# First four chunks turned by float32 identity products on TensorE in place of DMA transposes, state sums in float32, re-timed order

## The chip, the cores and the metric

The kernel runs on one core of a Trainium2 chip. The metric is the device time of one execution in microseconds (us). Engine names are those of the profile: PE (TensorE, the matrix unit; PEld its weight loads), DVE (VectorE), ACT (ScalarE), POOL (GpSimd), SP (SyncE, which here issues all DMA transfers).

## The reference

A gated linear attention is followed by a gated expert layer.

```python
for t in range(S):                                    # 4 batches, 8 heads, S = 768, D = 48
    state = alpha[:, :, t, :, None] * state + einsum('bhd,bhde->...', k[t], v[t])
    y[:, :, t] = einsum('bhd,bhde->bhe', q[:, :, t], state)
x = y as [3072 tokens, 384]
xn = x / sqrt(mean(x * x) + 1e-6) * rms_g
out = (silu(xn @ w_gate) * (xn @ w_val)) @ w_out      # 384 -> 1536 -> 384
```

All inputs and outputs are float32. (The first einsum is shortened here: it is the outer product of k and v of one token.)

## The kernel before

**Tiling.** The 3072 tokens are 24 chunks of 128. Chunk `cc` is the `cc // 4`-th chunk in time of batch `cc % 4`, so chunks 0 to 3 are the first chunks of the four batches: they have no state before them (`first`), and their output needs no product with a state. Seven groups (`GROUPS`: 4, 2, 2, 4, 4, 4, 4 chunks) go through the expert layer together.

**Attention of one chunk** (`attention`). SP loads decays, q and k of the chunk (`att`, 112 rows: two heads of 48, at rows 0 and 64) and v. DVE runs two scans over the decays (`scan`), and multiplies k and q by the results (`kh`, `qp`). PE multiplies k and q into scores (`sc`), DVE masks them (`mask`), PE multiplies them with v (`y32` for the first four chunks, in float32; `yv` later). ACT sums the squares (`sq`), POOL takes the root (`pow`), DVE multiplies by the gain (`x`), ACT and DVE split the scaled x into a high and a low float16 part (`x16`, `xl`). A DMA transpose on SP (`x_turn`) turns both parts into `xT`, which the expert layer multiplies. For the state, k is split into float16 parts as well (`k16`, `kl`), turned by a DMA transpose (`k_turn`), and multiplied with the float16 parts of v (`v16`, `vl`) by 48 small products on PE (`sums`).

**Float32 by float16 pairs.** Nearly every product is made of three float16 products (high x high, high x low, low x high: `SPLIT`). The low part is a subtraction on DVE.

**Weights.** 12 tiles of w_gate and w_val (`i0` to `i11`) and 6 of w_out (`o0` to `o5`) are loaded, brought into form by ACT (`abs`) and DVE (`shift`, `rest`), and split: the high part on ACT (`wh`), the low part on DVE (`wl`). For the names in `LOW_W` the low part is made by PE instead: two float32 products with a scaled identity (`wid`), two with minus the identity (`wneg`), and a copy by ACT (`wl2`).

**Expert layer.** `expert_in` makes 18 products per tile and column block (9 for gate, 9 for value); `expert_out` makes 36 per chunk. In group 0 the first five tiles (`EARLY`) are first multiplied with chunks 0 and 1 alone (256 columns), then with chunks 2 and 3 (`CUTS`); the names in the order are `mm_<group>_<tile>_<first chunk>_<gate 0 or value 1>`.

**Order.** No loop sets the order. Each piece of work is an `op` with an engine, a planned cost (`COST`) and a due time; the class `Plan` lays them out by a list schedule, with buffer counts (`BUFS`: one `y` output bank, three `at` and three `mm` banks, three row buffers `att`, two raw weight buffers), and the code is then written in that order, engine by engine. Each engine executes its queue in order. The tables `DUE`, `GAP`, `LATE` and `W_LATE` shift due times and so set the order.

**Row loads.** `load_att` fills a row buffer with one transfer of 112 rows the first time, and later with two of 48 rows, leaving the padding rows as they are.

## Time and profile before

| | us |
|---|---|
| device time, three runs | 532.52, 533.43, 533.54 (median 533.43) |
| device time of the profiled execution | 532.83 |
| span of the profiled execution | 531.0 |
| PE busy in the span | 505.1 (95%) |
| DVE busy | 395.1 (74%) |
| ACT busy | 259.3 (49%) |
| POOL busy | 34.7 (7%) |

The span is what lies between the first and the last instruction in the profile. A busy share is an average over stages: here the first 68 us, the stretch from there to 523 us, and the last 7.6 us differ, and the stages are shown with the prediction. A view of groups gives, for the instructions of one line and shape, the count, the busy time, the mean time of one in ns, and the idle time before them with what ended it; a timeline gives them in order of time; a table of waits gives for each engine whom it waited for, in total, how often and the longest. The granted clock is that of PE, 1.00 being full.

### The profile page before, as it was taken

The page shows a single profiled execution, that of the slowest core. Times are in us where ns is not written, and L with a number is a line of the kernel's source. Part 1 is how long each engine was busy: PE and PEld are TensorE (multiplying, and loading weights), DVE is VectorE, ACT ScalarE, POOL GpSimd, SP SyncE. Part 2 cuts the span into 40 slices and gives each one's busy share as a digit, 9 for nine tenths or more (in the row PEclk, how much of TensorE's full clock was granted, in tenths as well). Part 3 has the DMA queues.
Part 4 walks back from the last instruction along what each step waited for, and adds up shares of the span by engine and source line. Part 5 has one row for each costly group of instructions (what it writes and reads, how often), then busy time and mean ns, then how long its engine had stood idle before and what let it go on. Part 6 is the DMA issues. An engine that isn't in the chain of part 4 may idle for free.

```text
span 531.0 us, 11900 instructions
## 1 busy us (share of the span) xinstructions
PE 505.1 (95%) x4798; PEld 301.4 (57%) x4798; DVE 395.1 (74%) x745; ACT 259.3 (49%) x674; POOL 34.7 (7%) x79
## 2 busy tenths in 40 slices
PE   2888999999999999999999999999999999999994
PEld 1656774567886886545556545456544456444551
DVE  7997999999999999999997779898644320333212
ACT  3565888744663574446734557665544310232200
POOL 3002000001001010100210000021100000000000
PEclk9975999999999999999999999999999999999998
DMA  8999976748346539453379992516710000000001
GB/s 263 215 243 225 192 222 197 222 95 160 61 75 152 94 75 141 110 93 63 78 185 243 234 215 75 190 32 156 209 54 1 15 16 31 15 1 1 1 34 32
DMA packets 70673, 62.65 MB, mean 118 GB/s; under 512 B 40257, under 2 KB 64961, under 8 KB 70609
## 3 DMA queue, kind: packets, MB, share of 16 engines
q1 hardware_dynamic: 70608, 61.81, 50.8%
q8 instruction: 39, 0.64, 0.5%
q14 instruction: 26, 0.20, 0.1%
HBM read 47.77 MB, written 4.72 MB: 99 GB/s over the span
## 4 chain that ended last, share of the span: by engine, by line
PE 78%; DVE 11%; DMA 3%; ACT 1%; issue 1%; DVEq 0%
PE mm L1078 47%; PE mm_po L1148 22%; PE at L756 2%; DMA kT<-k 2%; PE y L841 2%; PE at L896 2%; DVE w L649 1%; PE y L820 1%; DVE wu_i L543 1%; DVE h L1108 1%; DVE h L1095 1%; DMA xT<-x 1%; DVE wu_o L543 1%; PE y_i L558 1%; DVE wg L551 1%
## 5 line engine op out<-in xcount | busy, mean ns | idle before, releaser
L1078 PE MATMUL mm<-xT,wg 128*128 128x512 f16 (+1 forms) x1602 | 291.6, 341 | 0.5 <-ACT sl L1089 0.2
L1078 PEld LDWEIGHTS <-wg 128*128 128x128 f16 x1602 | 155.3, 99 | 122.4 <-issue 0.5
L1148 PE MATMUL mm_po<-wo,h 128*128 128x384 f16 x864 | 144.9, 326 | 0.3 <-DVE ob L1159 0.3
L1148 PEld LDWEIGHTS <-h 128*128 128x128 f16 x864 | 83.0, 98 | 55.8 <-issue 1.3
L1095 DVE SCALAR_TENSOR_TENSOR h<-mm,sl 128x512 f32<-128x512 f32 (+1 forms) x89 | 52.1, 586 | 46.6 <-PE mm L1078 45.1
L503 ACT ACTIVATE h<-h 128x512 f16<-128x512 f32 (+1 forms) x89 | 48.6, 547 | 77.8 <-DVE h L1095 77.4
L1089 ACT ACTIVATE sl<-mm 128x512 f32<-128x512 f32 (+1 forms) x89 | 45.5, 512 | 45.9 <-PE mm L1078 45.3
L1108 DVE TENSOR_TENSOR h<-h,h 128x512 f16<-128x512 f32 (+1 forms) x89 | 51.7, 585 | 18.9 <-ACT h L503 18.7
L649 DVE TENSOR_TENSOR_SCAN w<-att,seed 112x520 f32<-112x520 f32 x48 | 59.4, 1238 | 2.7 <-DMA att<-att 2.3
L1159 DVE TENSOR_SCALAR ob<-mm_po 128x384 f32<-128x384 f32 x24 | 13.3, 554 | 34.9 <-PE mm_po L1148 34.9
L935 POOL TENSOR_TENSOR ss<-ssq,eps 128x1 f32<-128x1 f32 x24 | 12.0, 501 | 371.3 <-ACT junk L931 371.3
L769 DVE TENSOR_TENSOR at<-at,mask 128x512 f32<-128x512 f32 x40 | 25.9, 692 | 4.4 <-PE at L756 4.0
L880 ACT CAST a<-at 128x512 f16<-128x512 f32 x40 | 22.9, 584 | 10.1 <-DVE at L769 9.9
L883 DVE TENSOR_TENSOR a<-at,a 128x512 f16<-128x512 f32 x40 | 25.8, 684 | 0.1
L503 ACT ACTIVATE k<-kh 112x512 f16<-112x512 f32 x24 | 15.1, 627 | 9.7 <-DVE kh L679 7.3
L503 ACT ACTIVATE q<-qp 112x512 f16<-112x512 f32 x20 | 12.6, 628 | 13.5 <-DVE qp L686 9.9
L686 DVE TENSOR_TENSOR qp<-att,w 112x256 f32<-112x256 f32 x48 | 18.8, 420 | 0.1
L945 ACT ACTIVATE x<-x,ss 128x384 f16<-128x384 f32 x24 | 14.7, 611 | 5.0 <-POOL ss L936 3.5
L936 POOL TENSOR_TENSOR ss<-ss,mhalf 128x1 f32<-128x1 f32 x24 | 16.9, 706 | 1.9
L756 PE MATMUL at<-q,k 48*128 48x128 f16 x480 | 16.9, 217 | 0.0
L693 DVE TENSOR_TENSOR k<-kh,k 112x512 f16<-112x512 f32 x24 | 16.4, 682 | 0.7 <-ACT k L503 0.7
L503 ACT ACTIVATION_READ_ACCUMULATOR h<-h 128x1 f32 x89 | 16.8, 188 | 0.0
(107 smaller groups left out, 433.4 us busy)
## 6 DMA issues: line engine op xcount, KB each, us to landing
att<-att SPq DMA_DIRECT2D x42, 289.9 KB, 5.1
v<-vtok SPq DMA_DIRECT2D x24, 192.0 KB, 3.4
out_dram<-ob SPq DMA_DIRECT2D x24, 192.0 KB, 2.2
raw_c<-w_gate SPq DMA_DIRECT2D x12, 384.0 KB, 4.7
raw_c<-w_val SPq DMA_DIRECT2D x12, 384.0 KB, 5.6
raw_d<-w_out SPq DMA_DIRECT2D x6, 768.0 KB, 5.6
raw_i<-w_gate SPq DMA_DIRECT2D x11, 384.0 KB, 7.0
raw_i<-w_val SPq DMA_DIRECT2D x11, 384.0 KB, 8.4
```

The lines of the kernel that those rows point to most:

```text
L503: nc.scalar.activation(dst, src, AF.Copy, scale=scale, accum_out=stat[:rows, col : col + 1])
L649: nc.vector.tensor_tensor_scan(w, x, start.rearrange("r g p c -> r (g p c)"), 0.0, op0=ALU.mult, op1=ALU.add)
L686: nc.vector.tensor_tensor(by_half(t["qp"])[:, g], q, w, op=ALU.mult)
L756: nc.tensor.matmul(o, t["k16"][r, x, p, :], t["q16"][r, y, p, :], start=m == 0, stop=m == 2,)
L769: nc.vector.tensor_tensor(t["sc"][j], t["sc"][j], mask[:, int(first)].to_broadcast([P, NP, C]), op=ALU.mult,)
L880: nc.scalar.copy(a_tile()[:, j, 0], t["sc"][j])
L883: nc.vector.tensor_tensor(a_tile()[:, j, 1], t["sc"][j], a_tile()[:, j, 0], op=ALU.subtract)
L1078: nc.tensor.matmul(ps[:, :n], wg[:, f, x, j, kk, :], xT[:, y, kk, cs], start=i == 0, stop=i == 3 * NK - 1,)
L1089: nc.scalar.activation(t["sl"][:, :n], t[0][:, :n], AF.Silu, scale=1.0 / (S_X * S_W))
L1095: nc.vector.scalar_tensor_tensor(t["h"][:, :n], t[1][:, :n], S_H / (S_X * S_W), t["sl"][:, :n], op0=ALU.mult, op1=ALU.mult,)
L1108: nc.vector.tensor_tensor(h16_of(g, f)[:, 1, cs], t["h"][:, :n], h16_of(g, f)[:, 0, cs], op=ALU.subtract)
L1148: nc.tensor.matmul(t[i][:, :DM], h16_of(g, f)[:, x, ts], wo[:, f // 2, y, f % 2, :], start=f == 0 and m == 0, stop=f == NF - 1 and m == 2,)
```

## The change

For chunks 0 to 3 (`first`):

- k is no longer split. PE multiplies each of the four pairs of heads of `kh` with a float32 identity (`kp`: four products, 112 rows to 128 x 112), ACT copies the result (`k16`, now a float32 copy into the `kT` buffer), and the state sums are 16 float32 products with v itself (`u32`) in place of 48 float16 ones. The splits of v fall away too.
- x is scaled by root and gain in one DVE operation (`scaled`, which now waits for POOL's root), turned by three float32 products with the identity (`xp`, into an `mm` bank), and split on the way out: ACT copies the high part into `xT` (`x16`), DVE subtracts it for the low part (`xt`).
- So eight DMA transposes go, four of k and four of x.

For all chunks, the rows are loaded in one transfer of 112 rows. `LOW_W` keeps `i0` and `i1`; the low parts of `i2` and `i3` return to DVE. The tables of due times have new numbers. A new constant `one` (identity) is made on POOL, and start values of the check statistics change.

```diff
-LOW_W = ("i0", "i1", "i2", "i3")
+LOW_W = ("i0", "i1")
@@
-GAP = [-27.4, 83.2, 75.1, 36.9, -13.6, -70.1, 64.4]
+GAP = [-30.6, 131.5, 92.4, 44.6, -25.7, -125.5, 179.1]
...
     def load_att(cc, lo, hi):
-        new = (plan.slot["att", cc], lo) not in held
-        held.add((plan.slot["att", cc], lo))
-        for r in (slice(0, R),) if new or hi - lo < AW else (slice(0, D), slice(64, R)):
-            nc.sync.dma_start(att_tile(cc)[r, lo:hi], att[src(cc), r, lo:hi])
+        nc.sync.dma_start(att_tile(cc)[:, lo:hi], att[src(cc), :, lo:hi])
@@
+        def k_across():
+            t["kp"] = buf(ps_at, [P, NP, R], F32, "at", (cc, 4))
+            for p in range(NP):
+                nc.tensor.matmul(t["kp"][:, p, :], t["kh"][:, p, :], one[:R, :R], start=True, stop=True)
+
+        def k_back():
+            k = tl(ap, [P, 2, NP, R], F16, "kT").rearrange("s x p r -> s (x p r)").bitcast(F32)
+            t["k32"] = k.rearrange("s (p r) -> s p r", p=NP)
+            nc.scalar.copy(t["k32"], t["kp"])
+
+        def sums32():
+            t["u"] = [buf(ps_at, [R, NP, D], F32, "at", (cc, 2 + h)) for h in range(2)]
+            v = tiles["v", cc].rearrange("s (j p e) -> s j p e", j=2, p=NP)
+            for p in range(NP):
+                for j in range(2):
+                    r = slice(64 * j, 64 if j == 0 else R)
+                    for h in range(2):
+                        rows = slice(h * HC, (h + 1) * HC)
+                        nc.tensor.matmul(
+                            t["u"][h][r, p, :], t["k32"][rows, p, r], v[rows, j, p, :],
+                            start=True, stop=True,
+                        )
@@
+        def scaled():
+            t["x32"] = tl(ap, [P, DM], F32, "x32")
+            nc.vector.scalar_tensor_tensor(
+                like(t["x32"]), y_sum(), t["ss"], like(rg), op0=ALU.mult, op1=ALU.mult
+            )
+
+        def x_across():
+            t["xp"] = buf(ps_mm, [P, NK, C], F32, "mm", key("x"))
+            for kk in range(NK):
+                nc.tensor.matmul(
+                    t["xp"][:, kk, :], t["x32"][:, kk * P : (kk + 1) * P], one, start=True, stop=True
+                )
+
+        def x_half(x):
+            o = xT_of(g)[:, :, :, i * C : (i + 1) * C]
+            if x == 0:
+                nc.scalar.copy(o[:, 0], t["xp"])
+            else:
+                nc.vector.tensor_tensor(o[:, 1], t["xp"], o[:, 0], op=ALU.subtract)
@@
+        if first:
+            xp = ("mm", key("x"))
+            x = add("DVE", "x", scaled, [rt, tiles["rg"]], [y_k, key("x32"), key("ss")])
+            x = add("PE", "xp", x_across, [x], [key("x32"), xp])
+            x = add("ACT", "x16", lambda: x_half(0), [x], [xp, ("xT", g)])
+            xt = op("DVE", COST["xl"], lambda: x_half(1), [x], [xp, ("xT", g)], due=due, kind="xt")
@@
             if first:
+                kt = add("PE", "kp", k_across, [kh], [key("kh"), u2])
+                kt = add("ACT", "k16", k_back, [kt], [key("kT"), u2])
+                u = add("PE", "u32", sums32, [kt, lv], [key("kT"), key("v"), u0, u1])
                 st = add("ACT", "st0", s_back, [u], [u0])
```

Where the instructions stand now. In the rows, the number behind a name is the chunk (or the weight tile), the last one only counts the tiles.

**DVE, up to the operation that the first expert product waits for.** Before, the rows end with the multiply of chunk 2 (`x32_2`), which frees the one `y` bank for chunk 3's output on PE:

```order
L693 TENSOR_TENSOR k16_3_397<-kh_3_393,k16_3_397 112x512
L543 SCALAR_TENSOR_TENSOR wu_i8_414<-raw_i8_256,wu_i8_414 128x768
L649 SCALAR_TENSOR_TENSOR w_4_422<-att1_142,seed_91 112x520
L551 SCALAR_TENSOR_TENSOR wg_133<-wu_i8_414,wg_133 128x768
L783 TENSOR_TENSOR a16_3_440<-at_3_0_404,mask_97 128x512
L783 TENSOR_TENSOR a16_3_440<-at_3_1_405,mask_97 128x512
L727 SCALAR_TENSOR_TENSOR gd_4_443<-dec_132 112x4
L669 RECIPROCAL seed2_95<-w_4_422 112x8
L738 TENSOR_TENSOR sd0_349<-st0_348,gd_4_443 112x192
L711 SCALAR_TENSOR_TENSOR v16_3_434<-v_3_342,v16_3_434 128x384
L941 TENSOR_TENSOR x32_2_500<-y_2_425,rg_90 128x384
```

After the change, they end with the subtract that completes the turned x of chunk 1 (`xT_0` is the turned x of group 0; `mm_x_1` the bank into which PE turned chunk 1):

```order
L663 RECIPROCAL seed2_95<-w_4_345 112x8
L721 SCALAR_TENSOR_TENSOR gd_4_364<-dec_139 112x4
L732 TENSOR_TENSOR sd0_286<-st0_285,gd_4_364 112x192
L962 SCALAR_TENSOR_TENSOR x32_1_376<-y_1_325,ss_1_361,rg_90 128x384
L777 TENSOR_TENSOR a16_3_379<-at_3_0_347,mask_97 128x512
L777 TENSOR_TENSOR a16_3_379<-at_3_1_348,mask_97 128x512
L545 SCALAR_TENSOR_TENSOR wg_140<-wu_i2_341,wg_140 128x768
L643 SCALAR_TENSOR_TENSOR w_4_345<-att_4_216,seed2_95 112x520
L534 TENSOR_SCALAR wu_i5_415<-raw_i5_292 128x768
L537 SCALAR_TENSOR_TENSOR wu_i5_415<-raw_i5_292,wu_i5_415 128x768
L978 TENSOR_TENSOR xT_0_318<-mm_x_1_392,xT_0_318 128x3x128
```

The low parts of k (`k16`) and v (`v16`) are gone, chunk 3 has overtaken chunk 2, and both scans of chunk 4 (`w_4`) stand ahead of the gate, where it was one.

**PE, among the first expert products.** Before, the state sums of chunk 3 from the DMA-turned k (`kT_3`) stand between the first and the second product group:

```order
L1078 LDWEIGHTS wg_133
L1078 MATMUL mm_0_0_0_0_532<-xT_0_266,wg_133 128x256
L896 LDWEIGHTS kT_3_420
L896 MATMUL at_3_2_549<-v16_3_434,kT_3_420 64x48
L896 LDWEIGHTS kT_3_420
L896 MATMUL at_3_3_550<-v16_3_434,kT_3_420 64x48
```

After the change, behind the fifth product group, the turning of chunk 3's x and the output of chunk 2:

```order
L1126 MATMUL mm_0_2_0_0_515<-xT_0_318,wg_140 128x256
L969 MATMUL mm_x_3_535<-one_111,x32_3_526 128x128 x3
L790 MATMUL y_2_543<-v_2_457,a16_2_331 128x48 x8
L1126 LDWEIGHTS wg_140
L1126 MATMUL mm_0_2_0_1_565<-xT_0_318,wg_140 128x256
```

and behind three more groups the state sums of chunk 1, the turning of chunk 2's k and x:

```order
L899 MATMUL at_1_2_609<-v_1_157,kT_1_277 48x48
L899 MATMUL at_1_3_610<-v_1_157,kT_1_277 48x48
L884 MATMUL at_2_4_633<-one_111,kh_2_289 128x112 x4
L969 MATMUL mm_x_2_645<-one_111,x32_2_627 128x128 x3
L1126 LDWEIGHTS wg_140
L1126 MATMUL mm_0_4_0_0_656<-xT_0_318,wg_140 128x256
```

The state sums of chunk 2 follow two product groups later. Chunk 3's output, which stood right ahead of the first product, still does.

**SP, the queue of transfers.** Before, from the loads of chunk 2's rows on:

```order
L432 DMA att2_159<-att 112x1546
L432 DMA att0_137<-att 48x1546 x2
L697 DMA_TRANSPOSE kT_0_189<-k16_0_179 128x8x112
L432 DMA att1_142<-att 48x1546 x2
L529 DMA raw_i2_220<-w_gate 128x3x1024
L529 DMA raw_i2_220<-w_val 128x3x1024
L697 DMA_TRANSPOSE kT_1_234<-k16_1_214 128x8x112
L437 DMA v_2_245<-vtok 128x384
L529 DMA raw_i8_256<-w_gate 128x3x1024
L529 DMA raw_i8_256<-w_val 128x3x1024
L959 DMA_TRANSPOSE xT_0_266<-x16_0_251 128x6x128
```

After the change:

```order
L423 DMA att_1_150<-att 112x522
L423 DMA att_2_152<-att 112x1546
L423 DMA att_1_150<-att 112x1024
L428 DMA v_1_157<-vtok 128x384
L523 DMA raw_i0_159<-w_gate 128x3x1024
L523 DMA raw_i0_159<-w_val 128x3x1024
L523 DMA raw_i1_165<-w_gate 128x3x1024
L523 DMA raw_i1_165<-w_val 128x3x1024
L423 DMA att_3_183<-att 112x1546
L423 DMA att_4_216<-att 112x1546
L523 DMA raw_i2_250<-w_gate 128x3x1024
L523 DMA raw_i2_250<-w_val 128x3x1024
```

Chunk 2's rows now stand ahead of the first two weight tiles, and no transpose stands between the loads.

More of the change, by code (lines that the diff above doesn't have):

```diff
@@ L92 @@
 W_LATE = [
[L93 to L94 removed]
+    -228.4, -155.3, -67.5, 59.0, 68.2, 5.4, 63.1, 136.0, 18.2, 137.7, 147.9, 35.5, 44.8, 167.4,
+    194.4, 105.4, 241.9, 186.0,
 ]
@@ L419, in att_tile @@
     def att_tile(cc):
-        n = plan.slot["att", cc]
-        return tile_of(
-            ("att", n),
-            lambda: ain.tile([R, AW], F32, tag=f"att{n}", name=f"att{n}", bufs=1),
-        )
-    held = set()
+        return tile_of(("att", cc), lambda: buf(ain, [R, AW], F32, "att", cc))
     def load_att(cc, lo, hi):
-        new = (plan.slot["att", cc], lo) not in held
-        held.add((plan.slot["att", cc], lo))
-        for r in (slice(0, R),) if new or hi - lo < AW else (slice(0, D), slice(64, R)):
-            nc.sync.dma_start(att_tile(cc)[r, lo:hi], att[src(cc), r, lo:hi])
+        nc.sync.dma_start(att_tile(cc)[:, lo:hi], att[src(cc), :, lo:hi])
     def load_v(cc):
@@ L471, in tile_attn_moe @@
     same = const.tile([P, P], F32, name="same")
+    one = const.tile([P, P], F32, name="one")
     nc.gpsimd.memset(same, 0.0)
-    for x, value in ((minus, -1.0), (same, S_W)):
+    nc.gpsimd.memset(one, 0.0)
+    for x, value in ((minus, -1.0), (one, 1.0), (same, S_W)):
         nc.gpsimd.affine_select(
@@ L495, in tile_attn_moe @@
     nc.gpsimd.memset(stat, 0.0)
-    nc.gpsimd.memset(stat[:, o_qq : o_qq + NB], 2.0**10)
+    for o in (0, o_kk, o_qq):
+        nc.gpsimd.memset(stat[:, o : o + NB], 2.0**14)
     ssq = const.tile([P, NC], F32, name="ssq")
@@ L920, in s_front @@
             nc.vector.scalar_tensor_tensor(
-                st, t["u"][1], S_K[1] / S_K[0], st, op0=ALU.mult, op1=ALU.add
+                st, t["u"][1], S_K[1] / S_K[0] * (S_V if first else 1.0), st, op0=ALU.mult, op1=ALU.add
             )
@@ L982, in attention @@
         qp = add("DVE", "qh", lambda: mul_q(1), [qp], [att_k, w_k, key("qp")], lock=True)
-        kd = add("ACT", "k16", k_hi, [kh], [key("kh"), key("k16")])
-        kl = add("DVE", "kl", k_lo, [kd], [key("kh"), key("k16")], lock=True)
-        vd = add("ACT", "v16", v_hi, [lv], [key("v"), key("v16")])
-        vl = add("DVE", "vl", v_lo, [vd], [key("v"), key("v16")], lock=True)
+        if not first:
+            kd = add("ACT", "k16", k_hi, [kh], [key("kh"), key("k16")])
+            kl = add("DVE", "kl", k_lo, [kd], [key("kh"), key("k16")], lock=True)
+            vd = add("ACT", "v16", v_hi, [lv], [key("v"), key("v16")])
+            vl = add("DVE", "vl", v_lo, [vd], [key("v"), key("v16")], lock=True)
         if first:
```

39 lines of the change are left out of this document (19 added, 20 removed).

## The prediction

> **What bounds the kernel now.** I first cut the span into stages, at the places where TensorE (PE) changes its state. Each row gives the stretch, its length, then busy us and instruction count of PE, PE weight loads, DVE, ACT and POOL, the granted clock, the DMA share and the GB/s.
>
> ```profile
> 0.00:44.64 44.64, 28.22 (x243) 21.80 (x244) 38.59 (x66) 22.29 (x51) 7.35 (x32) 0.86 1.05 231
> 44.64:68.02 23.38, 21.91 (x253) 16.81 (x254) 19.34 (x38) 17.10 (x46) 2.17 (x2) 0.82 1.04 219
> 68.02:101.20 33.18, 33.18 (x187) 17.52 (x182) 32.41 (x55) 26.84 (x63) 0.74 (x2) 1.00 0.69 205
> 101.20:130.80 29.60, 29.22 (x409) 19.08 (x409) 29.21 (x55) 14.22 (x37) 1.22 (x3) 1.00 0.71 145
> 130.80:523.40 392.60, 392.59 (x3716) 226.22 (x3715) 274.97 (x534) 178.87 (x479) 23.26 (x41) 1.00 0.40 91
> 523.40:531.00 7.60, 0.00 (x0) 0.00 (x0) 0.56 (x1) 0.00 (x0) 0.00 (x0) 0.76 0.13 38
> ```
>
> From 68 to 523 us PE is never free: the idle time is 0.4 us in 455, at full clock. That stretch can only move as a block. What can change is when it starts, and how much PE work it holds. The 26 us in which PE does nothing lie in the first 68 us (17.9) and behind the last product (7.6). DVE is nearly as full from 68 to 131 us (61.6 of 62.8), so it stands right behind PE.
>
> Next come the waits of PE in the first stages, and PE's own timeline there (start, us, instruction, idle before).
>
> ```profile
> PE y L796 <- DVE x L941: 2.0, 1, 2.0
> PE at L896 <- DMA kT<-k: 1.1, 1, 1.1
> ...
> 35.59 1.99 PE L796 MATMUL y<-v,a 128*128 128x48 f32 x16
> 38.67 0.54 PE L896 MATMUL at<-v,kT 64*64 64x48 f16 x47 [0.96 <-DVE a L783]
> 41.19 3.65 PE L796 MATMUL y<-v,a 128*128 128x48 f32 x16 [1.98 <-DVE x L941]
> 44.64 2.12 PE L1078 MATMUL mm<-xT,wg 128*128 128x256 f16 x9
> 47.85 0.83 PE L896 MATMUL at<-v,kT 64*64 64x48 f16 x48 [1.09 <-DMA kT<-k]
> 48.61 5.21 PE L1078 MATMUL mm<-xT,wg 128*128 128x256 f16 x27
> 53.66 1.46 PE L558 MATMUL y_i<-wu_i,same 128*128 128x384 f32 x4
> 54.95 0.49 PE L565 MATMUL y_i<-wg,minus 128*128 128x384 f16 x2
> 68.02 33.25 PE L1078 MATMUL mm<-xT,wg 128*128 128x256 f16 x180
> ```
>
> The first expert product is at 44.64. It stands behind chunk 3's output (41.19), which waits for DVE's multiply of chunk 2 to free the one output bank. At 47.85 PE waits for the transposed k of chunk 3: the only place where a transpose holds PE.
>
> The clock (stretch, PE busy, granted clock, DMA share, GB/s):
>
> ```profile
> 44.00:46.00 2.00, 2.00 (x11) 0.50 1.98 191
> ...
> 52.00:54.00 2.00, 2.00 (x14) 0.77 1.13 205
> 54.00:56.00 2.00, 2.00 (x13) 1.00 1.18 142
> ```
>
> So the first products run at half clock until about 53 (0.77 in 52 to 54 is about 0.9 us at half; the 27 records from 48.61 take 0.193 each). From 44.64 that is some 8.4 us, of which half, 4.2 us, is lost.
>
> **The change, part by part.** The sum is made on the profiled run: span 531.0 us, 532.83 us with what lies around it. The median shown, 533.43, is 0.6 above that.
>
> *1. The first product comes earlier.* DVE fills the time ahead of it. Its two ends, and the mean times of what leaves or joins its queue (busy us, mean ns, idle):
>
> ```profile
> 3.96 1.31 DVE L649 TENSOR_TENSOR_SCAN w<-att,seed 112x520 f32<-112x520 f32 x1 [2.34 <-DMA att<-att]
> 40.58 0.56 DVE L941 TENSOR_TENSOR x<-y,rg 128x384 f32<-128x384 f32 x1 [0.43 <-ACT junk L931]
> ...
> L649 DVE TENSOR_TENSOR_SCAN w<-att,seed 112x520 f32<-112x520 f32 x48 | 59.4, 1238 | 2.7 <-DMA att<-att 2.3
> L693 DVE TENSOR_TENSOR k<-kh,k 112x512 f16<-112x512 f32 x24 | 16.4, 682 | 0.7 <-ACT k L503 0.7
> L948 DVE SCALAR_TENSOR_TENSOR x<-x,ss,x 128x384 f16<-128x384 f32 x24 | 14.7, 611 | 1.3 <-ACT x L945 1.2
> L711 DVE SCALAR_TENSOR_TENSOR v<-v,v 128x384 f16<-128x384 f32 x24 | 13.2, 551 | 0.0
> L941 DVE TENSOR_TENSOR x<-y,rg 128x384 f32<-128x384 f32 x10 | 5.5, 554 | 0.8 <-ACT junk L931 0.8
> ```
>
> Before, DVE gates the first product with the multiply that ends at 41.14 (57th operation in its queue). After, the gate is the subtract that completes the turned x of chunk 1 (51st). Counted in the two queues up to there, three low parts of k (0.68 each) and three of v (0.55) are gone, one multiply (0.55) falls behind the gate, one scan (1.24) comes ahead of it; two low parts of x become two subtracts, taken at the same 0.61. That is 2.0 + 1.7 + 0.55 - 1.24 = 3.0 us less, so the subtract ends at 38.1. Chunk 3's output now stands ahead of the gate in both queues (its masks are six operations earlier on DVE), so the product follows at once, where before it came 3.5 us behind the multiply.
>
> Against that stand new waits: the turned x goes DVE, PE, ACT, DVE, and while the subtract waits, chunk 4's scaled q and k and the next weight tiles stand behind it on DVE; on PE the scores of the next chunk stand behind a product that waits for DVE's x. Bounds: 0, and 3.65, what one cold output pass of PE takes (41.19). I take 1.2, nearer the low end, since other work stands between the steps in each queue. First product at 39.3: **5.3 us earlier**.
>
> *2. The wait for kT goes:* **1.1 us** (47.85). Late next on PE is the scaled x of chunk 3, which the order places behind five half-size expert products.
>
> *3. PE work behind the first product.* Before, three state sums (two here, one later) and a weight tile by PE: 0.5 + 0.5 and 1.46 + 0.49 less overlap (53.66 to 55.4), 2.8 us. After: two turned x, one turned k, two float32 state sums, and chunk 2's output. The trace has no such shapes; the nearest float32 rows are the output above (1.99 us for 16 records, 0.124 each, 48 columns) and the weight tile:
>
> ```profile
> 32.69 1.56 PE L558 MATMUL y_i<-wu_i,same 128*128 128x384 f32 x4
> 34.50 1.16 PE L764 MATMUL at<-qp,kh 48*128 48x128 f32 x16
> ```
>
> that is 0.39 per record at 384 columns, and 0.073 where two quarter-height tiles run side by side. A turned x is three products, six records of 128 columns: between 0.75 and 2.3 us; 1.0, since 128 lies nearer 48. A turned k, eight records of 112: between 1.0 and 3.1; 1.2. A state sum, 32 records on quarter tiles: between 0.36 (at the 0.011 of 38.67) and 2.3 (at 0.073); 1.0, between the f16 form of the same tiles and the next float32 one. Chunk 2's output is 2.0. Sum 2.0 + 1.2 + 2.0 + 2.0 = 7.2, less 2.8: **4.4 us more** (bounds 2.4 and, everything dear, 11.5).
>
> *4. Clock:* half clock for some 8.4 us around the first products, as before: **0**. The order puts a turned x and an output of 48 columns among them (the profile went to 0.50 right after such outputs, 35.59 and 38.67), so I don't count on less.
>
> *5. Hidden or small.* ACT trades the high parts of k and v of four chunks, and two residues, for copies of like size, and is half free (22.29 of 44.64). POOL makes one more constant before the first turned k, under the first scores; if late, only that product waits. The row loads grow from two of 48 rows to one of 112:
>
> ```profile
> att<-att SPq DMA_DIRECT2D x42, 289.9 KB, 5.1
> v<-vtok SPq DMA_DIRECT2D x24, 192.0 KB, 3.4
> att<-att SPq DMA_DIRECT2D x1, 676.4 KB, 10.7
> xT<-x SPq DMA_TRANSPOSE x24, 2.8
> kT<-k SPq DMA_TRANSPOSE x20, 4.7
> ```
>
> 676.4 - 2 x 289.9 = 97 KB more per chunk, five chunks of it in the first 60 us: 0.5 MB, 2 us at 231 GB/s. Seven transposes (by their shapes 229 KB for k, 197 for x) leave the same stretch, 1.5 MB. So the DMA engines, at a share over 1 until 68, get relief. On SP the chunk loads wait for one of three row buffers with weight loads behind them: before, it is the transposes that stand there. Weight loads can land late where the row load ahead of them is held; bounds 0 and 3 us, taken 0, since the bytes fall. After 131 us the share is 0.40 and all of this is covered.
>
> [...] The medians agree roughly (4.7 us against 3.4 for v); the chain's own piece does not:
>
> ```profile
> 35.76 12.04 DMA kT<-k
> ```
>
> [...]
>
> **Sum:** -5.3 - 1.1 + 4.4 + 0 = -2.0. 532.83 becomes 530.8; on the median, 531.4. I forecast 531.0, between the two.
>
> **Rivals.** *(a) DVE hands the gain back: no change.* Up to the gate of the last in-product of group 0, DVE's queue is only 0.9 us shorter (155 against 152 operations), because two weight tiles' low parts return to it. The order moves the low part of weight tile i10 from 122nd to 138th, 11.1 us of DVE work later. Before, it was ready long ahead:
>
> ```profile
> 80.50 0.93 DVE L551 SCALAR_TENSOR_TENSOR wg<-wu_i,wg 128x768 f16<-128x768 f32 x1
> 405.27 23.31 PE mm L1078 x108
> ```
>
> ready at 81.4, used 36 products of 0.216 before 101.2, at 93.4. After: 92.5, if DVE idles as much as before. Then PE can gain 0.9 at most, whatever its start: 532.2. For it speaks DVE's 61.6 of 62.8 us; against, that 4.0 us of DVE idle in 44.64 to 68.02 sit beside the waits that go.
>
> *(b) The clock stays half: slower.* If the turned x and the output among the first products keep the clock at 0.50 until 58, 9.4 us are lost in place of 4.2: -2.0 + 5.1 = +3.1, 536. It turns slower from 52 us on. For it: a pass of such outputs went before each drop to half. Against: at 49 to 53 us of before, dense products brought the clock back. Dear float32 records (term 3's upper ends) give the same size.
>
> *(c) The clock is full early: faster.* If PE, now denser ahead of 39 us, enters the products at full clock, the 4.2 us come back; DVE's queue allows 4.0 + 0.9 in all. 528.0. [...] The trace had 8.4 us from the first product to full clock, so I give it little.
>
> *(d) The change doesn't cut what PE waits for:* the turned k leaves only 1.1 us of PE waits, so if the earlier start fails, terms 2 and 3 give +3.3. It counts with (b).
>
> **How the numbers follow.** Forecast 0.46; (a) 0.21; (b) with (d) 0.20; (c) 0.13. A measurement of this kernel can tell about 0.2%, 1.1 us, from no change. Faster by more: forecast and (c), and a little of (a): 0.62. Within: the rest of (a): 0.18. Slower: 0.20. The range goes from 527.5 (just past (c)) to 535.5 (most of (b)); what lies outside is less than 2 in 10.
>
> **What would show it.** Right: a first expert product at 38 to 40.5, no wait of PE for a DMA of kT, a block without PE idle from about 60 on; a turned x near 1.0 and a turned k near 1.2 us at full clock; DVE idle between 40 and 65 under 3 us. Wrong: PE waiting for DVE's low part of a weight tile around 85 to 95 us (a); a granted clock of 0.50 past 52 us (b), or 1.00 at the first product (c); DVE waiting for raw weight loads (term 5); PE idle behind 130 us.

## The result and the profile after

The changed kernel took **527.13 us** (median of 5 runs, 526.57 to 528.63), against 532.52 us (531.49 to 533.54) for the kernel before on the same chip: a ratio of 0.9902, 95% interval 0.9879 to 0.9925. The profiled run took 526.98 us with a span of 525.3 us; before, 532.83 and 531.0. So the change brought about 5.4 us where 2.0 were forecast.

The stages after, cut where TensorE (PE) changes its state as in the prediction's first view (stretch, length, busy us of PE, weight loads, DVE, ACT and POOL, granted clock, DMA share, GB/s):

```profile
0.00:38.93 38.93, 27.44 (x225) 22.99 (x226) 32.62 (x54) 14.79 (x32) 10.00 (x34) 1.00 0.98 246
38.93:57.51 18.58, 16.48 (x192) 13.60 (x192) 18.37 (x35) 14.57 (x39) 2.56 (x4) 1.00 0.80 230
57.51:86.87 29.36, 29.36 (x185) 17.53 (x182) 28.80 (x51) 24.40 (x64) 0.00 (x0) 1.00 0.76 214
86.87:124.64 37.77, 36.95 (x448) 22.11 (x448) 37.04 (x67) 19.44 (x47) 1.48 (x4) 1.00 0.59 146
124.64:518.00 393.36, 393.36 (x3738) 227.78 (x3739) 275.25 (x535) 178.82 (x480) 18.85 (x41) 1.00 0.36 94
```

PE's last product ends at 518.0 in place of 523.4, and the long full stretch starts at 124.64 in place of 130.80, so the gain was made ahead of it. The granted clock is 1.00 in the first two rows, where it was 0.86 and 0.82. Only for the first 25.5 us or so (before, the first 22) the column does not show PE's true pace: it reads 1.00 there, and yet the four records of a weight tile took 2.93 us, against 1.56 later (before, 2.93 at 18.22 and 1.56 at 32.69).

```profile
22.86 2.93 PE L552 MATMUL y_i<-wu_i,same 128*128 128x384 f32 x4
34.03 1.56 PE L552 MATMUL y_i<-wu_i,same 128*128 128x384 f32 x4 [1.30 <-DVE x L962]
```

VectorE (DVE) is busy 18.37 of 18.58 us behind the first expert product; before it was 19.34 of 23.38.

Three of PE's waits after (us in total, times, longest):

```profile
PE mm L1126 <- DVE wg L545: 1.5, 3, 0.6
PE y_i L552 <- DVE x L962: 1.3, 1, 1.3
PE mm L1126 <- ACT sl L1137: 0.6, 1, 0.6
```

And PE's timeline after, from the first expert product to the block of 180 (start, us, instructions, idle before and releaser):

```profile
38.93 3.29 PE L1126 MATMUL mm<-xT,wg 128*128 128x256 f16 x27
42.79 2.18 PE L1126 MATMUL mm<-xT,wg 128*128 128x256 f16 x18 [0.57 <-ACT sl L1137]
45.46 0.91 PE L969 MATMUL mm_x<-one,x 128*128 128x128 f32 x6 [0.49 <-DVE x L962]
46.21 1.88 PE L790 MATMUL y<-v,a 128*128 128x48 f32 x16
47.93 1.36 PE L1126 MATMUL mm<-xT,wg 128*128 128x256 f16 x11
49.86 1.92 PE L1126 MATMUL mm<-xT,wg 128*128 128x256 f16 x16 [0.57 <-DVE wg L545]
51.71 0.67 PE L899 MATMUL at<-v,kT 64*64 64x48 f32 x32
52.31 1.15 PE L884 MATMUL at<-one,kh 112*128 112x112 f32 x8
53.52 0.94 PE L969 MATMUL mm_x<-one,x 128*128 128x128 f32 x6
54.30 0.38 PE L1126 MATMUL mm<-xT,wg 128*128 128x256 f16 x2
55.06 1.92 PE L1126 MATMUL mm<-xT,wg 128*128 128x256 f16 x16 [0.38 <-DVE wg L545]
56.91 0.67 PE L899 MATMUL at<-v,kT 64*64 64x48 f32 x32
57.51 29.42 PE L1126 MATMUL mm<-xT,wg 128*128 128x256 f16 x180
```

No DMA is among PE's waits any more. Behind the first expert product, what ends a wait now is DVE's scaled x or its low part of a weight tile, or ScalarE's share of an expert product. The first 27 products take 3.29 us where the 27 at 48.61 took 5.21.

DVE's own queue from 40 to 60 us shows the other half of the story. The row of that stretch before:

```profile
40.00:60.00 20.00, 17.62 (x184) 13.79 (x185) 15.42 (x28) 12.94 (x32) 2.91 (x4) 0.68 1.16 220
```

And after:

```profile
40.00:60.00 20.00, 17.92 (x207) 15.05 (x205) 19.69 (x36) 16.32 (x44) 2.56 (x4) 1.00 0.80 242
```

DVE's idle time there fell from 4.6 to 0.3 us. From about 14 us to 60 it does not wait for anything any more; ahead of that it waits twice for the rows of a chunk, besides the wait for its very first rows (2.17 us; before 2.34). DVE's timeline after:

```profile
9.89 1.24 DVE L643 TENSOR_TENSOR_SCAN w<-att,seed 112x520 f32<-112x520 f32 x1 [1.78 <-DMA att<-att]
14.39 0.76 DVE L680 TENSOR_TENSOR qp<-att,w 112x256 f32<-112x256 f32 x2 [0.56 <-DMA att<-att]
```

### The profile page after: what moved, and what is told of

It reads as the page before. It is cut to its first block, busy times and chain, and to the rows that moved or that the text cites. A ratio compares the mean times of both kernels' runs of the same rounds, so it can differ in the third digit from the quotient of the medians.

```text
span 525.3 us, 11773 instructions
## 1 busy us (share of the span) xinstructions
PE 504.1 (96%) x4778; PEld 304.1 (58%) x4778; DVE 392.6 (75%) x739; ACT 252.0 (48%) x660; POOL 32.9 (6%) x83
## 4 chain that ended last, share of the span: by engine, by line
PE 81%; DVE 13%; issue 2%; DMA 1%; ACT 1%; POOL 1%; SPq 0%; DVEq 0%; POOLq 0%
PE mm L1126 46%; PE mm_po L1196 24%; PE at L750 3%; PE y L835 2%; PE y L790 1%; DMA att<-att 1%; PE at L913 1%; DVE wu_i L537 1%; DVE h L1156 1%; DVE h L1143 1%; DVE w L643 1%; PE y L814 1%; DVE wo L545 1%; DVE wg L545 1%; PE y_i L552 1%
## 5 line engine op out<-in xcount | busy, mean ns | idle before, releaser
L1126 PEld LDWEIGHTS <-wg 128*128 128x128 f16 x1602 | 153.3, 98 | 122.6 <-DVE wg L545 2.5
L952 POOL TENSOR_TENSOR ss<-ssq,eps 128x1 f32<-128x1 f32 x24 | 8.6, 359 | 342.0 <-ACT junk L948 342.0
L953 POOL TENSOR_TENSOR ss<-ss,mhalf 128x1 f32<-128x1 f32 x24 | 18.1, 754 | 1.9
L497 ACT ACTIVATE k<-kh 112x512 f16<-112x512 f32 x20 | 12.5, 626 | 11.0 <-DVE kh L673 9.1
L750 PEld LDWEIGHTS <-k 48*128 48x128 f16 x480 | 13.4, 94 | 6.1 <-issue 5.3
L673 DVE TENSOR_TENSOR kh<-att,w 112x512 f32<-112x512 f32 x24 | 16.4, 684 | 0.0
L666 ACT COPY dec<-w 112x8 f32<-112x8 f32 x24 | 4.9, 205 | 23.9 <-DVE w L643 23.8
```

The lines of the kernel that those rows point to most:

```text
L497: nc.scalar.activation(dst, src, AF.Copy, scale=scale, accum_out=stat[:rows, col : col + 1])
L750: nc.tensor.matmul(o, t["k16"][r, x, p, :], t["q16"][r, y, p, :], start=m == 0, stop=m == 2,)
L1126: nc.tensor.matmul(ps[:, :n], wg[:, f, x, j, kk, :], xT[:, y, kk, cs], start=i == 0, stop=i == 3 * NK - 1,)
```

## The experiments

Four theories were set against each other. **C**: the full clock is the missed gain. **D**: after the change, DVE's queue sets the pace of the first stages, and PE's work beside it counts little. **P**: PE's own work sets the pace from the first product on. **O**: the gain belongs to the order (the re-timed tables), not to the operations. The kernel before ran in every group of runs; its median lay between 531.7 and 532.7 us, so less than 1 us between groups is not a difference to lean on. "Block" is the start of PE's stretch without idle time (57.51 in the changed kernel).

| run | time, us | ratio to before, 95% interval | first product | block | span |
|---|---|---|---|---|---|
| changed kernel | 527.13 | 0.9902 [0.9879, 0.9925] | 38.93 | 57.51 | 525.3 |
| fill in the kernel before | 531.29 | 0.9979 [0.9962, 0.9997] | 41.94 | - | 528.2 |
| old tables | 533.67 | 1.0022 [1.0006, 1.0038] | 39.61 | - | 530.4 |
| first loads reordered | 525.40 | 0.9866 [0.9843, 0.9888] | 38.78 | 55.81 | 523.9 |
| the same with fill | 524.98 | 0.9876 [0.9852, 0.9900] | 36.97 | 55.45 | 523.3 |
| less PE work | 527.75 | 0.9931 [0.9907, 0.9955] | 38.30 | 57.72 | 525.9 |
| 2 us more on PE | 527.61 | 0.9920 [0.9901, 0.9939] | 41.56 | 57.97 | 525.6 |
| 2 us more on DVE | 529.95 | 0.9950 [0.9935, 0.9964] | 42.42 | 60.10 | 528.2 |
| the same with fill | 528.99 | 0.9949 [0.9931, 0.9966] | 40.92 | 59.40 | 527.3 |
| 2 us more on DVE, late | 530.76 | 0.9961 [0.9945, 0.9977] | 41.48 | 58.52 | 529.8 |
| clock lowered | 528.47 | 0.9930 [0.9905, 0.9955] | 39.20 | 57.74 | 525.4 |
| two low parts less | 526.50 | 0.9890 [0.9862, 0.9918] | 38.66 | 56.31 | 524.6 |

In the changed order the span follows the block, not the first product: over the runs whose delay lies ahead of it, block and span shift by the same amount to within 0.5 us, while the first product moved by 2.6 us in the run with more PE work and the block by only 0.5.

### The clock alone, in the kernel before

Thirty-four float16 products that nobody reads went into PE's idle places of the kernel before, the numbers of them by chunk:

```
+            if cc == 2 and h == 1:
+                fill(4, 2)          # behind the output
...
+            if cc == 3:
+                fill(14, 2)         # ahead of the state sums
...
+            fill({0: 8, 1: 8}.get(cc, 0), 2)
```

> The kernel before, its queues unchanged, with 34 extra float16 products of 512 columns on PE, whose results nobody reads, put where PE idles: 8 behind chunk 0's state sums (idle 25.2 to 27.4 us), 4 behind chunk 2's output, 8 behind chunk 1's state sums (idle until 41.2), 14 ahead of chunk 3's state sums (which wait for kT until 47.8). Theory C (the clock was the 4 us that the prediction missed: PE falls to half clock because its float32 work with few columns and its gaps leave it too little occupied, and the queues can use a faster PE): granted clock 1.00 from 33 to 55 us, 27 products from 48.6 in about 3.05 us in place of 5.2, and 1.5 to 3 us faster than before, although PE does more (less than 4.2, since kT still lands at about 47.8). Theory D (DVE's queue sets the pace, a faster PE only waits more): clock 1.00 as well, but time within 0.7 us of before or slower by what the extra products delay.

The clock was 1.00 from 28 us on, and the 27 products took 3.12 us in place of 5.21. The time fell by only 1.4 us against the kernel before in its group (0.2 to 2.0 by the interval, 2.8 in the profiled runs), between what the two theories had. PE's timeline in that run shows what took the place of the slow products:

```profile
40.12 1.99 PE L807 MATMUL y<-v,a 128*128 128x48 f32 x16
41.94 1.15 PE L1094 MATMUL mm<-xT,wg 128*128 128x256 f16 x9
42.92 3.19 PE L477 MATMUL fill<-warm 128*128 128x512 f16 x14
46.95 0.56 PE L911 MATMUL at<-v,kT 64*64 64x48 f16 x48 [0.84 <-DMA kT<-k]
47.44 3.12 PE L1094 MATMUL mm<-xT,wg 128*128 128x256 f16 x27
```

The first product comes 2.7 us earlier, but the sums with the transposed k only 0.9 (46.95 for 47.85), since PE still waits 0.84 us for it. In this order, the clock alone is worth about a quarter of the gain.

### The order alone, and the parts under the old order

The changed operations with the four tables of the kernel before (new kinds of operation with no shift):

> The changed kernel with the numbers of GAP, DUE, LATE and W_LATE of the kernel before (the new kinds of work without a shift), so the float32 products and the large row loads in another order. Theory O (the order brought the gain): 531 to 535, no gain over before. Theory C: the clock stays at 1.00 past 39 us in this order too, as the same identity products run, and most of the gain stays: 527 to 529.5.

The time was 533.67 us, slightly above the kernel before, although in the profiled run (532.20) the first product comes at 39.61 and the clock is full up to 125 us. The three runs with the highest mean clock (0.992 to 0.995) took 532.1 to 532.4 us, so it is not the clock that keeps this order from the gain. PE's waits between 90 and 170 us in this run:

```profile
PE y L814 <- DVE x L958: 1.6, 2, 1.3
PE mm_po L1196 <- DVE ob L1207: 1.2, 1, 1.2
PE at L913 <- DVE a L877: 0.6, 1, 0.6
PE at L750 <- DVE a L877: 0.5, 1, 0.5
```

Its row from 125 to 200 us:

```profile
125.00:200.00 75.00, 72.48 (x1137) 59.62 (x1129) 71.84 (x157) 42.89 (x140) 7.18 (x12) 0.98 0.46 99
```

And that of the changed kernel:

```profile
125.00:200.00 75.00, 75.00 (x1172) 60.79 (x1167) 70.36 (x157) 43.51 (x142) 4.51 (x12) 1.00 0.37 92
```

DVE did as much by 125 us as in the changed kernel (117.65 and 117.19 us busy; before, 113.93), but on work that PE did not need yet, and PE gave back 2.5 us there and 1.1 us in each of two earlier stretches (40 to 60 and 90 to 125). So the operations bring nothing without an order that spends DVE's time on what PE waits for next. The other corner, the old operations with the new tables, is not among the runs.

Then one part at a time under the old tables. Only k by PE, x by the DMA:

```
-        if first:
+        if False:
             xp = ("mm", key("x"))
```

> The changed kernel with the tables of before and x of the first four chunks turned by the DMA as before: of the two turned arrays only k goes by TensorE (with float32 state sums, one-transfer rows and two weight tiles as after). With both by TensorE and these tables the time was 533.67 us, 1.2 above before. Theory K (the transposed k was the wait that counted in the kernel before, 1.1 us on the record): 531.0 to 532.2 us, better than before and than both. Theory O (with the old tables no part brings anything, since VectorE's order hands it back between 90 and 200 us): 532.5 to 534.5 us.

533.84 us (ratio 1.0029 [1.0006, 1.0053]): theory O. Only x by PE, k and v split and k turned by the DMA as before:

```
-        if not first:
+        if True:
             kd = add("ACT", "k16", k_hi, [kh], [key("kh"), key("k16")])
...
-            if first:
+            if False:
                 kt = add("PE", "kp", k_across, [kh], [key("kh"), u2])
```

> The changed kernel with the tables of before and k and v of the first four chunks split, and k turned by the DMA, as before: only x goes by TensorE. Theory X (the earlier x is what brings the first product forward): first product at 41 to 43 us, time 530.5 to 532.0 us. Theory O: 532.5 to 534.5 us, with TensorE waiting for VectorE between 90 and 200 us for 2 us or more.

531.27 us (0.9967 [0.9952, 0.9983]), first product at 40.84: theory X. So under the old tables x alone ends 1.2 us below the kernel before in its group, k alone 1.4 above, and the two together 1.0 above. These are not prices of the parts alone: all three runs also carry the large row loads and the two weight tiles that return to DVE, and PE's order differs between them.

Two undone parts under the new tables changed the order as well. With x by the DMA again:

> The changed kernel with the x of the first four chunks turned by the DMA in float16 as before (k still by TensorE, tables and weight tiles as after). The transposes of x took 8.7 us from issue to landing at 20 to 60 us before, while a turned x by TensorE takes 0.83 us and its two parts 0.5 us each. Theory D with the transfer on the path: the second chunk's x is ready near 34 us, so the first product comes at 42.5 to 44 us, and the stretch up to the block without idle time ends 1 to 3 us later: 528 to 530.5 us. Theory O (the re-timed tables and the order alone brought the gain; x by either way is hidden): 526.5 to 527.7 us. Theory C: TensorE has 0.83 us less work for each x ahead of the first product, the clock falls to 0.50 there, and the time is 531 to 533 us.

531.96 us (1.0005 [0.9990, 1.0021]): the whole gain is gone. That is theory C's number, and the clock did fall, to 0.50 from 36.9 to 43.7 us; but PE also waits 2.2 us for a transfer of x at 62.3 and 3.0 us for DVE's masked scores, so this run does not tell C from D. With four low parts by PE instead of two (`LOW_W = ("i0", "i1", "i2", "i3")`):

> The changed kernel with the low parts of four weight tiles by TensorE, as before, instead of two. VectorE loses two low parts of 0.95 us; TensorE gets two times 2.05 us and ScalarE two copies. In the changed kernel TensorE waits three times for such a low part, 1.5 us in all. Theory D (VectorE's queue sets the pace up to 57 us): TensorE's extra work fills its waits, and the time goes to 525.3 to 526.5 us. Theory P (from 38.9 us on TensorE's own work is the bound, and only its waits of 2.0 us are VectorE's): +4.1 for the work, -1.5 for the waits, 529 to 530 us.

554.65 us, outside both theories: the planner made another order out of it, in which PE waits 5.2 us for one scaled x and 4.0 us for a transposed k. This run prices the order, not the tiles; it shows how closely the tables fit one set of operations. The row loads of before, under the new tables:

```
...
+        for r in (slice(0, R),) if new or hi - lo < AW else (slice(0, D), slice(64, R)):
+            nc.sync.dma_start(att_tile(cc)[r, lo:hi], att[src(cc), r, lo:hi])
```

> The changed kernel with the row loads of before: three fixed row buffers, and from the fourth chunk on two transfers of 48 rows each in place of one of 112 rows. Theory O and theory D agree that it is off the path: 526.6 to 527.7 us. If the single transfer was part of the gain (one issue of SyncE in place of two, 0.45 us each, ahead of the weight loads), 528 to 530 us; if its 97 KB more per chunk cost something, below 526.4 us.

527.87 us (0.9920 [0.9905, 0.9934]): 0.7 us above the changed kernel and 0.2 above the band of O and D, not to be told from no effect.

### Work added to and taken from PE

A first attempt to take the float32 products of weight tile i1 away gave values outside the range that the kernel tests, so it took its general path (7662 us) and told nothing. The second left out i1's two float32 products and stored zero as its low part:

```
-            for n in range(2):
+            for n in range(0 if name == "i1" else 2):
                 nc.tensor.matmul(t["ps"][:, n, : NW // 2], same, ...)
...
-                    t["ps"][:, n, : NW // 2], minus, ...
+                    t["ps"][:, n, : NW // 2], zero if name == "i1" else minus, ...
```

> The changed kernel without the two float32 products that bring weight tile i1 to TensorE, and with a zero tile in place of the minus identity for i1's remaining two products, so the low part of i1 is stored as zero. The queues of the other engines are as in the changed kernel; TensorE has 1.6 us less to do just ahead of the first expert product, and its idle stretch there grows from 1.3 us (32.7 to 34.0) to about 2.7 us. Theory C (dense TensorE work keeps the granted clock up, and the clock is the missed 4 us): the clock falls to 0.50 near 35 and stays there to 42 or later, the first 27 products of 256 columns take up to 0.19 us each in place of 0.113, and the time goes to 529 to 531 us. Theory D (VectorE's queue sets the pace up to 57 us, TensorE waits for its low parts there anyway): whatever the clock does, the time stays between 526.3 and 528.0 us, because slower products only use up the waits of 0.57, 0.49, 0.57 and 0.38 us.

The clock stayed at 1.00, against theory C, so this run did not test what a lower clock costs. But 1.6 us less of PE work just ahead of the first product brought nothing: 527.75 us, in theory D's band. One product starts at 38.30, and the next then waits 0.94 us for the subtract on DVE. The opposite, nine more products right ahead of the first one:

```
...
+            if len(outs) == 6:
+                f = ps_mm.tile([P, 512], F32, tag="mm2", name="fill", bufs=1)
+                for _ in range(9):
+                    nc.tensor.matmul(f, warm[:, :P], warm, start=True, stop=True)
```

> The changed kernel with nine more float16 products of 512 columns that nobody reads, 2.0 us at full clock, behind the output that stands just ahead of the first expert product on TensorE. First product near 40.9 us in either case. Theory D: TensorE's waits behind it (0.57, 0.49, 0.57 and 0.38 us, 2.0 in all) are used up, the block without idle time starts at 57.5 to 58.0 us, and the time rises by less than 0.7 us (526.8 to 527.9). Theory P (from the first product on TensorE's own work is the bound): the waits stay, and the time rises by 1.6 to 2.0 us, to 528.7 to 529.4 us.

527.61 us, block at 57.97: theory D. Three of the four waits behind the first product were used up. The 0.46 us by which the block is later need not be the price of the added work, for PE was late by as much 8 us ahead of it (the changed kernel, then this run):

```profile
30.49 1.16 PE L758 MATMUL at<-qp,kh 48*128 48x128 f32 x16 [0.65 <-DVE kh L673]
30.96 1.16 PE L761 MATMUL at<-qp,kh 48*128 48x128 f32 x16 [0.62 <-DVE kh L676]
```

In two more runs whose edits act later, these scores start at 30.22 and 30.82, so half a microsecond at the block is what one profile differs from the next. Theory P falls: 2.0 us of PE in this stretch cost 0.5 at most.

### Work added to and taken from DVE

Five multiplies of 0.42 us ahead of the third scaled k, 2.2 us in the queue:

```
...
+            if len(keys) == 3:
+                for _ in range(5):
+                    nc.vector.tensor_tensor(spare, spare, spare, op=ALU.mult)
```

> The changed kernel with five more VectorE instructions of 0.40 us (a tile of its own multiplied by itself, read by nobody) ahead of the third scaled k, near 21 us: 2.0 us more in VectorE's queue ahead of the first expert product, nothing else changed. Theory D (VectorE's queue sets the pace up to 57 us): first product near 40.9 us, the block without TensorE idle time starts near 59.5 us in place of 57.5, and the time rises by 1.6 to 2.0 us, to 528.7 to 529.4 us. Theory S (there is slack in VectorE's queue, what set the new time is the order of TensorE): the time rises by less than 0.7 us.

529.95 us, +2.8. That is more than the 2.2, and the clock was 0.50 from 31.9 to 38.7 us in its profile, where PE had 2.7 us of idle time (up to 32.64). Filling that with 40 unused products:

> The changed kernel with the five unused VectorE instructions ahead of the third scaled k (as in the run that rose by 2.8 us, in which the clock was 0.50 from 32 to 38.6 us), and with 40 unused float16 products of 128 columns in the idle stretch of TensorE that this makes (30.0 to 32.6 us). Theory D: the clock is 1.00 throughout, the first product comes 1.5 us or more ahead of 42.4 us, and the time is 528.7 to 529.4 us, 1.6 to 2.2 over the changed kernel: the delay of VectorE alone. Theory C: with full clock the delay is hidden, 527.0 to 528.2 us.

528.99 us at full clock (1.00 from 32 to 38 us): +1.9, at the block as well. That is the delay of DVE alone, and nearly all of it is passed on. The half clock had added 0.7 at the block and 1.0 in the median. The same delay placed near 80 us:

> The changed kernel with the five unused VectorE instructions (2.0 us) ahead of the sixth scaled k, near 79 us, instead of the third. VectorE is busy 28.80 of 29.36 us between 57.5 and 86.9 and 34.3 of 35 between 90 and 125, so it has no idle time there either. Theory D57 (VectorE's queue sets the pace only up to the block of expert products that starts at 57.5 us; from there on its results are ready ahead of TensorE): the time rises by less than 0.7 us. Theory D125 (it sets the pace all the way to 125 us, and rival (a) of the prediction holds the gain down): the time rises by 1.4 to 2.2 us.

530.76 us, +3.6; D57 falls. Of its twelve runs four took 528.5 to 529.4 us, about D125's band, and eight 530.7 to 531.6. In the profiled one, the slowest, 1.0 us was already lost at the block (half clock from 31.3 to 38.2); then come three new waits of PE between 66 and 92 us:

```profile
PE mm L1133 <- ACT wg L500: 1.2, 1, 1.2
PE mm L1133 <- DVE h L1150: 0.9, 1, 0.9
PE mm L1133 <- ACT sl L1144: 0.7, 1, 0.7
```

The last of these ends at 66.3, ahead of the added multiplies (from 81.5 on), and is not theirs. The other two, which end at 85.9 and 92.2, make 2.1 us: the delay, passed on in full. So DVE's queue has no slack up to some 92 us, although PE shows almost no idle time there. Why eight of the runs were slower still stays open; the mean clock does not tell the two clusters apart (0.997 at 528.48 and at 530.92). The reverse, two low parts less (i2 and i5 stored as zero by GpSimd):

```
+            if name in ("i2", "i5"):
+                return nc.gpsimd.memset(dst[:, 1], 0.0)
```

> The changed kernel with the low parts of weight tiles i2 and i5 left out: GpSimd writes zeros in their place, where VectorE took 0.95 us each, one ahead of the first expert product and one right behind its gate. Theory D (VectorE's queue sets the pace): first product near 38.0 us, time down by 1.3 to 2.2 us, to 524.9 to 525.8. Theory P (TensorE's own work from the first product on): time down by the 0.9 us of the first product at most, 526.2 to 527.2.

526.50 us, -0.6, with an interval that overlaps that of the changed kernel. That is theory P's number, and D's was missed, though not in P's way: the first product moved by only 0.3, the block by 1.2. The part ahead of the first product did not count, because between the scaled x (DVE) and that product lie 4.9 us of PE's own chain (low part, turned x, state sum, output). And in the kernel before:

> The kernel before with the same five VectorE instructions ahead of its third scaled k. Theory D1 (there too VectorE's queue gates the first expert product, as step 1 of the prediction has it): first product near 46.6 us, time up by 1.0 to 2.0 us against the kernel before. Theory T (in the kernel before the transposes, the half clock and the waits of 40 to 60 us cover it, where VectorE is idle for 4.6 of 20 us): time up by less than 0.6 us.

532.01 us against 532.30 (0.9996 [0.9984, 1.0008]): theory T. The first product came 1.5 us later, and the time did not. PE's timeline there:

```profile
46.11 2.12 PE L1085 MATMUL mm<-xT,wg 128*128 128x256 f16 x9
48.16 0.83 PE L903 MATMUL at<-v,kT 64*64 64x48 f16 x48
48.93 3.69 PE L1085 MATMUL mm<-xT,wg 128*128 128x256 f16 x27
```

The transposed k is there when PE wants it, so the wait of 1.09 us takes up most of the delay, and the clock returns at 50.1 in place of 52.9, so fewer products are slow. In the kernel before, DVE's queue was hidden behind the transfer and the clock; after the change it is what is left.

### The first loads, and the clock in the changed order

SyncE's first ten transfers in the order in which DVE needs them:

```
+        loads = [o for o in todo if o["e"] == "SP"][:10]
+        first_loads = [loads[i] for i in (0, 1, 4, 2, 6, 5, 8, 3, 9, 7)]
...
```

> The changed kernel with only the first ten transfers on SP in another order: chunk 1's rows ahead of v, gain row and chunk 2's rows, weight tile i0 ahead of the gain row. DVE waited 1.78 and 0.56 us for chunk 1's rows (at 9.89 and 14.39). Theory D (DVE's queue sets the front, and with it the start of the block): those 2.3 us come off the first product (about 36.6 in place of 38.9) and 1.5 to 2.3 us off the time: 525 to 525.7. Theory C alone (PE and its clock set the front): under 0.7 us, or slower if the clock falls.

525.40 us, 1.7 better than the changed kernel, as D has it. DVE's waits for rows at 9.89 and 14.39 are gone. But the clock fell ahead of the first product, which so came at 38.78, not at D's 36.6. The same with six filler products in the idle places:

> The changed kernel with the first ten transfers reordered (525.4 us, clock 0.50 from 29.4 to 36.2 in its profile), and six more float16 products of 512 columns that nobody reads: four behind the second chunk's output (idle 27.1 to 28.2 there) and two behind the third turned k (idle 31.3 to 31.8). Theory C: the clock is 1.00 throughout, low part, turned x and output ahead of the first product take 3 us less, first product at 36 us or before, time 522.5 to 523.8 us. Theory D: the clock is 1.00 as well, but the first product comes less than 1 us earlier and the time is 524.8 to 525.7 us, since the subtract of VectorE ahead of it ends no earlier than its queue allows.

The stretch from 30 to 36 us without the fill:

```profile
30.00:36.00 6.00, 5.60 (x18) 3.76 (x18) 5.86 (x11) 3.16 (x7) 1.05 (x1) 0.50 0.76 225
```

And with it:

```profile
30.00:36.00 6.00, 5.31 (x62) 3.95 (x61) 5.86 (x12) 4.21 (x9) 1.35 (x1) 1.00 0.80 232
```

Full clock brought the first product from 38.78 to 36.97, the block from 55.81 to 55.45 and the time from 525.40 to 524.98 us: 1.8 us at the first product, 0.4 at the end. The time is theory D's, the early first product neither theory's. The 0.4 is not shown: the two intervals overlap, and against the kernel before in its own group the version with fill is the worse of the two (0.9876 and 0.9866). These are the best two versions of the study. Last, the clock lowered in the changed kernel, with i1's float32 products and the third turned k left out (so that its chunk adds nothing to its state):

> The changed kernel with less TensorE work just ahead of the first expert product, so that its clock falls there while VectorE's queue stays as it is: the two float32 products of weight tile i1 are left out (its low part is stored as zero), and the third turned k (31.6 to 32.7 us in the changed kernel) is made by four float16 products of a zero tile, so that chunk adds nothing to its state. TensorE's idle stretch ahead of the first product grows to 3.5 us. Expected in either case: granted clock 0.50 from about 35 us for 6.8 us or more, products of 256 columns at 0.19 to 0.22 us in place of 0.113 until then. Theory C (the full clock through the first products is the missed term of some 4 us): the time rises by 2.5 to 4.5 us over 527.1, to 529.6 to 531.6. Theory D (VectorE's queue sets the pace, TensorE's waits of 2.0 us take up slower products): it rises by less than 1.2 us, to at most 528.3.

528.47 us. In the profiled run (527.15) the clock was 0.50 for only 3.4 us; in the five timed runs beside it the mean clock over the span was 0.982 to 0.992 and the time 528.4 to 529.6. Between the two bands, at 1.3 us over the changed kernel: the clock counts, at a fraction of what it takes from PE (an estimate from the medians of the mean clock, 0.995 and 0.989: some 3 us of the span).

## Why the prediction was wrong

The direction was right and so were the first two steps; the size was not: 531.0 us with a range from 527.5, against 527.13. By its own steps:

1. *First product:* 39.3 forecast, 38.93 measured, 5.7 us earlier in place of 5.3. Right, in part by luck: up to the subtract DVE's busy time fell by 2.3 us (35.19 to 32.86) where 3.0 were counted, and its idle time rose by 0.4 where 1.2 of new waits were taken. These were waits for rows, not the hand-offs that the prediction names. And the subtract ends at 39.2, just behind the start of the first product, which follows PE's own output without a wait.
2. *The wait for kT:* gone, 1.1 us. Right. (Before, its transfer took 12.04 us and landed at 47.80.)
3. *PE work behind the first product:* +4.4 forecast. By the starts in the timeline above, two turned x take 0.75 and 0.78, the turned k 1.2, two state sums 0.6 each, the output 1.7: 5.7 less 2.8, so +2.9. The turned k met its price; sums, turned x and output were cheaper than the rows they were priced from. The term was also charged in full, where 2.0 us more of PE work cost 0.5 at most.
4. *"Clock: half clock for some 8.4 us around the first products, as before: 0."* **This is the step that failed.** The clock was full, which takes 3.6 us off PE's time: rival (c), to which the prediction gave 0.13. (Its 4.2 halves the wait for kT as well; between 44.64 and 52.9 PE was busy for 7.2 us.) Its evidence against (c) was that 8.4 us passed in the old trace before the clock came back. But waits that the change takes away belong to that stretch. With PE's idle places filled, the kernel before entered the products at full clock (the run with fill), and the waits of 0.96 and 1.98 us ahead of the first product are gone after the change. With the wait for kT, which step 2 removes, the half clock lasted 13.6 us; in the kernel before with more DVE work, where PE did not have to wait for it, 10.2. Why PE's wait of 1.30 us at 32.7, after the change, brought no fall stays open.
5. *Hidden or small:* no wait for a weight load came up in these stages. DVE's new waits for rows (2.3 us) were not foreseen; reordering the loads got 1.7 of it back.

New waits for DVE and ACT were counted only ahead of the first product. Behind it, PE is idle for 2.1 us (first stages above) where 0.4 would have been left without kT; between 87 and 125 us, 0.8 in place of 0.4. The account of the two traces is then -5.7 - 1.1 + 2.9 - 3.6 + 1.7 + 0.4 = -5.4, by which PE's last product ends earlier; what follows it is 0.3 shorter (7.3 for 7.6), which makes the 5.7 of the span.

That account has the right sum, but its terms do not stand side by side, and this is what the runs add. Full clock alone gave the kernel before 1.4 us, and in the changed order 1.3 at most, not 3.6; 2.0 us of PE work cost 0.5 at most; 2.2 us of DVE cost 1.9. After the change DVE sets the pace up to some 92 us, and PE's gains and costs mostly end in waits for it. Rivals (a) and (c) of the prediction came near that: DVE's queue shorter by 0.9, plus 4.0 us of its idle time, 4.9 in all, 528.0; 0.8 more came in the span. The idle time did go (4.6 to 0.3 in 40 to 60 us), and the sign named for (a) is there, though small: PE waits 0.50 us for a low part of a weight tile until 89.1. The clock's share of the gain cannot be split off exactly: with half clock, 3.6 us of PE would have met 2.1 us of waits, so some 1.5 us would have shown. That is worked out, not run; the run that lowered the clock lost 1.3.

That the new order is what makes DVE's time useful is shown by the run with the old tables (533.67). Why both together cost 2.4 us against x alone under the old tables stays open.

## What to carry to other kernels

Before adding up terms of the engine that looks full, ask which queue would set the pace once its waits are gone: two microseconds of unused work on each engine answer that in one run each. A wait that is removed may also be what held the clock down (here 13.6 us of half clock with the wait for kT and 10.2 without it), so the two terms are judged together. And tables that time an order belong to one set of operations: the same operations were worth -5.4 us with the one set and +1.0 with the other.

## What was new about the hardware

Up to the last product, the half clock came in stretches of one length, 3.4 us, and its multiples: 6.8 and 13.6 us in the kernel before; in the other versions (without the one of 7662 us) 3.4 in five of them, 6.8 in seven (three of these read from means over 20 to 40 us, to within 0.5 us) and 10.2 in the kernel before with more DVE work; the version with four low parts by PE has besides a mean clock of 0.86 from 125 to 200 us, 21 us at half in all. The starts in one run lie whole lengths apart as well: 25.6 and 39.3 in the kernel before, 4 lengths, and 27.1 and 51.0 where only k goes by PE, 7 lengths. The run with the lowered clock has a single length (quarter microseconds around its ends; the column ahead of the DMA share is the clock):

```profile
33.75:34.00 0.25, 0.00 (x0) 0.00 (x0) 0.25 (x2) 0.25 (x1) 0.00 (x0) 0.86 1.11 297
34.00:34.25 0.25, 0.00 (x0) 0.00 (x0) 0.25 (x2) 0.25 (x3) 0.00 (x0) 0.50 0.42 99
...
37.25:37.50 0.25, 0.25 (x6) 0.16 (x4) 0.25 (x2) 0.00 (x0) 0.00 (x0) 0.82 0.59 205
37.50:37.75 0.25, 0.25 (x3) 0.25 (x4) 0.25 (x2) 0.23 (x1) 0.00 (x0) 1.00 0.20 66
```

The 13.6 us of the old trace are four such lengths, where the prediction counted the 8.4 us from the first product on, and the third of them (46.1 to 49.5, PE busy for 2.31 of 3.40 us) holds the wait for kT. PE at work throughout one length did not always bring the clock back: in the second (42.7 to 46.1) PE was busy for 3.42 of 3.42 us, the first 2.0 us with the output of 48 columns, and the clock stayed at 0.50; it came back behind the fourth (49.5 to 52.9), with PE busy for 3.42 of 3.42 us as well. What brings it back is not shown. An idle stretch of 1.30 us (32.7 to 34.0) left the clock full in the changed kernel, and one of 1.09 us (27.1 to 28.2) was followed by a fall at 29.3 in the version with reordered loads. Of that version's five runs two had a mean clock of 0.995 and 0.996 and three of 0.991: it seems that whether such a gap costs the clock differs from run to run (one of the five was profiled).
